# Decay attention and two MLPs on one core: masks by scans, fewer filling products in the chunk loop, operand splits ahead of weight groups

## The chip, the cores and the metric

The kernel runs on one core of one Trainium2 chip. The metric is the device time of one execution in microseconds. Engines are named as in the profile: PE is TensorE's matrix multiply and PEld its weight load, DVE is VectorE, ACT is ScalarE, POOL is GpSimd, SP is SyncE, which here issues nearly all DMAs.

## The reference

Attention with a decay per head over 2 batches, 8 heads, 768 positions and 64 channels, then two MLPs over the 1536 tokens of width 512. Everything is float32.

```python
# attention, block by block (the state runs over the blocks)
Dmask = where(i >= j, lam_h ** (i - j), 0)
out   = ((q k^T) * Dmask) v  +  (q * lam ** (i + 1)) state
state = lam ** block * state + (k * lam ** (block - 1 - i))^T v
# first MLP (d_ff 1536), then second MLP (d_ff 2048)
x = (sigmoid(x @ w_gate) * (x @ w_val)) @ w_out
x = elu(x @ w_in) @ w_out2
```

## The kernel before, in words

**Attention.** The positions are cut into six chunks of 128 (`NCH` = 6, `CH` = 128), for all heads and both batches. Two tables are made at the start, both in one SBUF tile that the trace calls `low`: `da` holds the decay mask of each head (128 x 128, eight heads, 128 x 1024 in all), and `lp` the powers of lam along the positions. Keys and values are stored with their positions reversed, so a mask is constant along anti-diagonals: entry (row r, column n) depends on r + n alone. Before the change each head's mask is read out of one row: DVE builds a row of powers for each head (`pw`, 8 partitions x 256), ACT's queue writes it to DRAM (`rows`, L296), and a DMA on SP's queue (L297) reads it back, each partition from one element further, into `da`, 512 KB.

For chunk c the pieces are: `front_mm` (L325, scores `st` for one batch, 16 matmuls), `front_post` (L331, DVE multiplies scores by `da` into `pr`), `front_pre` (ACT scales keys into `kd`, L314; POOL scales queries into `ql`, L318), `state_mm` (L338, 32 matmuls into `u`), `state_post` (DVE, `sn`), `out_mm` (L355 and, from the second chunk on, L360, into `x`, and an ACT copy `xa`). Then `build_from_psum` turns the attention output of the chunk straight into the operands of the first MLP: "11" and "22" (ACT and DVE, L171 and L172), sums (DVE, L176 and L178), and the splits of the sums into a high and a low part, "143" and "P" (ACT L181, POOL L182).

**First MLP.** Each 512 x 512 product of weights and tokens is done in blocks by seven products (M1 to M7, a Strassen scheme). One product here is a call of `step`: six matmuls of 256 columns at L209 into one of three PSUM banks A, B, C, and an eviction. A bank is taken again by the next pair as soon as its last eviction is done. A pair G (gate) or V (value) is the seven products M2, M5, M1, M4, M3, M7, M6 for one set of tokens.

**Filling products.** The pairs G and V of the first weight group are done in three parts of 256 columns: part 1 is ready after chunk 1, part 2 after chunk 3, part 3 after chunk 5. Each part puts 14 products into the list `fills`. Inside the chunk loop `fill(k)` takes k products from the list, between attention's own matmuls. What is left goes out after the loop (`fill(len(fills))`, L508). Before any product is ready, in chunks 0 and 1, `warm_up` matmuls on zeros stand there.

**Order of the work.** In the attention part PE and SP run in the written order (`manual_schedule`). The other engines, and PE after the loop, are ordered by a planner that simulates the program when it is built and takes what is ready by priority; `tc.high_priority(offset=HP)` puts instructions ahead of ordinary ones. The chunk loop's own work is in such a block, and so are the first half of `build_from_psum` and the fills. The preparation of weight groups (`prep_pair`: L71 to L73 unpack, L81 to L85 sums on POOL, L91 and L92 splits) has ordinary priority, and so have the "143" and "P" splits of `build_from_psum` (L181, L182). The split weights have two buffers of each kind, so the next gate group is split only when the first gate group has been used for the last time.

**SP's queue** in written order: lam, chunk 0, the masks (L297, waits for `rows`), the first gate weights (L61), chunks 1 and 2, the first value weights, chunks 3, 4 and 5.

Of the kernel before, what the change touches and what calls it, by code (L numbers as in the profile page):

```python
# [7 lines left out]
F32 = mybir.dt.float32  # L8
# [4 lines left out]
ALU = mybir.AluOpType  # L13
PSUM = bass.MemoryType.PSUM

P = 128
B, H, S, D = 2, 8, 768, 64
NP = H // 2
CH = 128
# [3 lines left out]
NS = (256, 512)  # L23
FG = 256
TB = 256
HP = 1000
# [4 lines left out]
def tile_decay_attention_two_mlps(  # L31
# [11 lines left out]
    nc = tc.nc  # L43
# [5 lines left out]
    sig_p = ctx.enter_context(tc.tile_pool(name="sig", bufs=1))  # L49
# [113 lines left out]
    def build_from_psum(ops, s, x0, x1, xa, t0, n, sums):  # L163


        sl = slice(t0, t0 + n)
        o = ops[s]
        a, b = slice(0, 2), slice(2, 4)
        with tc.high_priority(offset=HP):
            for key, src in (("11", x0[:, a]), ("22", x1[:, b])):  # L170
                nc.scalar.copy(o[key, "h"][:, :, sl], src)  # L171
                nc.vector.tensor_tensor(out=o[key, "l"][:, :, sl], in0=src, in1=o[key, "h"][:, :, sl].bitcast(F32),  # L172
                                        op=ALU.subtract)
            for k, (i0, i1, op) in enumerate(((x1[:, b], xa[:, a], ALU.add), (x0[:, b], xa[:, a], ALU.subtract),
                                              (x1[:, a], xa[:, 4:6], ALU.subtract))):
                nc.vector.tensor_tensor(out=sums[:, k], in0=i0, in1=i1, op=op)  # L176
            t = t_p.tile([P, 512], F32, tag="xt", name="xt", bufs=3).rearrange("p (k n) -> p k n", k=KC)
            nc.vector.tensor_tensor(out=t, in0=x1, in1=xa[:, 0:KC], op=ALU.add)  # L178
        for key, src, view in (("143", sums, (slice(None),) * 3), ("P", t, (slice(None),) * 2)):
            hi_, lo_ = (o[key, q][view + (sl,)] for q in "hl")  # L180
            nc.scalar.copy(hi_, src)  # L181
            nc.gpsimd.tensor_tensor(out=lo_, in0=src, in1=hi_.bitcast(F32), op=ALU.subtract)  # L182


    t2_p, ps1_p = [], []
# [60 lines left out]
    with ExitStack() as actx:  # L246
        a2_p = actx.enter_context(tc.tile_pool(name="a2", bufs=2))
        ap_p = actx.enter_context(tc.tile_pool(name="ap", bufs=1, space=PSUM))
        dr_p = actx.enter_context(tc.tile_pool(name="dr", bufs=1, space=bass.MemoryType.DRAM))

        start = ExitStack()
        start.enter_context(tc.manual_schedule(engines={mybir.EngineType.PE, mybir.EngineType.SP}))
# [2 lines left out]
        low = acc_p.tile([P, 2, KC, NS[0]], F32, tag="acc0", name="low").rearrange("p a k n -> p (a k n)")  # L255
        nat = acc_p.tile([P, 2, KC, NS[1]], F32, tag="acc1", name="nat").rearrange(
            "p a k n -> p (a k n)").rearrange("p (z b q h e) -> p z b q h e", z=2, b=2, q=2, h=H)
        da = low[:, 0:1024].rearrange("p (q g n) -> p q g n", q=2, g=NP)
        lp = low[:, 1024:1536].rearrange("p (g n) -> p g n", g=NP)
        rev = da[:, :, :, CH - 1:CH]  # L260
        l_ch = lp[:, :, CH - 1:CH]


        lam_s = a2_p.tile([P, 1 + NP], F32, tag="lam", name="lam", bufs=1)
        nc.sync.dma_start(out=lam_s, in_=lam2)
        pw = sig_p.tile([P, 2, 2, NS[0]], F32, tag="sig0", name="pw").rearrange("p a h n -> p (a h n)")[0:H, 0:2 * CH]
        rows = dr_p.tile([H, 2 * CH], F32, name="rows")

        tin, nat_of = {}, {c: nat[:, int(c in (1, 4))] for c in (0, 1, 3, 4, 5)}

        def load(c, halves=False):
            if c == 2:
                tin[c] = xop_p.tile([P, KC, NS[1]], F32, tag="xPh1", name="tin2").rearrange(
                    "p k n -> p (k n)").rearrange("p (b q g s) -> p b q g s", b=2, q=2, g=NP)
                nat_of[c] = sig_p.tile([P, 2, 2, NS[1]], F32, tag="sig1", name="nat2").rearrange(
                    "p a h n -> p (a h n)").rearrange("p (b q h e) -> p b q h e", b=2, q=2, h=H)
            else:
                tin[c] = a2_p.tile([P, 2, 2, NP, CH], F32, tag="tin", name="tin")
            to = tin[c].rearrange("p b q g s -> p b (q g s)")
            for b in (slice(0, 1), slice(1, 2)) if halves else (slice(0, 2),):  # L280
                nc.sync.dma_start(out=to[:, b], in_=att[c, 0][:, b])
            nc.sync.dma_start(out=nat_of[c].rearrange("p b q h e -> p b (q h e)"), in_=att[c, 1])

        load(0, True)
        nc.vector.memset(pw[:, 0:CH - 1], 0.0)
        nc.vector.memset(pw[:, CH - 1:CH], 1.0)
        nc.vector.memset(pw[:, 2 * CH - 1:2 * CH], 0.0)
        nc.vector.tensor_copy(pw[:, CH:CH + 1], lam_s[0:H, 0:1])
        n = 1
        while n < CH // 2:  # L290
            nc.vector.tensor_tensor(out=pw[:, CH + n:CH + 2 * n], in0=pw[:, CH:CH + n],
                                    in1=pw[:, CH + n - 1:CH + n].to_broadcast([H, n]), op=ALU.mult)
            n *= 2
        nc.vector.tensor_tensor(out=pw[:, CH + n:CH + 2 * n - 1], in0=pw[:, CH:CH + n - 1],
                                in1=pw[:, CH + n - 1:CH + n].to_broadcast([H, n - 1]), op=ALU.mult)
        nc.scalar.dma_start(out=rows, in_=pw)  # L296
        nc.sync.dma_start(out=da.rearrange("p q g n -> p (q g) n"),  # L297
                          in_=bass.AP(tensor=rows.tensor, offset=rows.offset, ap=[[1, CH], [2 * CH, H], [1, CH]]))
        nc.vector.tensor_copy(lp[:, :, 0], lam_s[:, 1:1 + NP])
        n = 1  # L300
        while n < CH:
            nc.vector.tensor_tensor(out=lp[:, :, n:2 * n], in0=lp[:, :, 0:n],
                                    in1=lp[:, :, n - 1:n].to_broadcast([P, NP, n]), op=ALU.mult)
# [29 lines left out]
        def state_mm(c):  # L333
            u = us[c] = ap_p.tile([P, 2, NP, D], F32, tag="u", name="u", bufs=1)
            for b in range(2):
                for p in range(NP):
                    for q, r in ((0, lo), (1, hi)):
                        nc.tensor.matmul(u[r, b, p], lhsT=kds[c][:, b, 2 * p + q], rhs=nat_of[c][:, b, 1, 2 * p + q],  # L338
                                         start=True, stop=True)

        def state_post(c):
            u = us[c]
            sn = sns[c + 1] = a2_p.tile([P, 2, NP, D], F32, tag="sn", name="sn")
            if c == 0:
                nc.vector.tensor_copy(sn, u)
            else:
                for p in range(NP):
                    nc.vector.scalar_tensor_tensor(out=sn[:, :, p], in0=sns[c][:, :, p], scalar=l_ch[:, p],
                                                   in1=u[:, :, p], op0=ALU.mult, op1=ALU.add)
# [22 lines left out]
        def fill(k):  # L372
            for _ in range(k):
                if fills:
                    fills.pop(0)()
# [6 lines left out]
        def warm_up(k):  # L382
            for _ in range(k):
                nc.tensor.matmul(warm, lhsT=idle[:, :P], rhs=idle, start=True, stop=True)
# [10 lines left out]
        for c in range(NCH):  # L395
            if c == 0:
                wV = prep_pair(w_val, 0, nc.gpsimd, nc.gpsimd)
            more = c + 1 < NCH
            with tc.high_priority(offset=HP):
                if more:  # L400
                    state_mm(c)
                    state_post(c)
                    front_pre(c + 1)
                fill(2)
                for b in range(2):
                    out_mm(c, b)
                    if c <= FIRST[0]:
                        warm_up(3)
                    fill(2)
                    if more:  # L410
                        front_mm(c + 1, b)
                        front_post(c + 1, b)
                    if c <= FIRST[0]:
                        warm_up(3)
                    fill(1 + b)
                if c + 3 < NCH and c < 2:
                    load(c + 3)
                if c == 3:
                    load(c + 2)
            if c == 1:  # L420
                xops += new_xops(1)
                sig = new_sig()
                pG = Pair("G", wG, xops, sig)
                pV = Pair("V", wV, xops, sig)
            s, t0 = (0, c * CH) if c < 2 else (1, (c - 2) * CH)
            build_from_psum(xops, s, xps[c, 0], xps[c, 1], xas[c], t0, CH,
                            a2_p.tile([P, 3, 2, CH], F32, tag="sums", name="sums"))
            if c in FIRST:
                r = PARTS[FIRST.index(c)]
                fills += [lambda q=q, m=m, r=r: step(q, m, r) for q in (pG, pV) for m in ORDER]  # L430
# [78 lines left out]
    g = new_g()  # L509
# [8 lines left out]
    for i in range(1, NG1 - 1):  # L518
# [11 lines left out]
        g = new_g()  # L530
# [15 lines left out]
    g = new_g()  # L546
# [27 lines left out]
    for i in range(NG2):  # L574
# [29 lines left out]
        if last:  # L604
            a = ws_p.tile([P, 1024, 2], U32, tag="w64", name="o64").rearrange("p (t n) x -> p t (n x)", t=4).bitcast(F32)
            b = ws_p.tile([P, 1024], F32, tag="w32", name="o32").rearrange("p (t n) -> p t n", t=2)
# [57 lines left out]
```

## Time and profile before

| | |
|---|---|
| time, median of 3 runs | 634.04 us (634.03 to 635.12) |
| the profiled execution | 633.13 us, its span on the core 631.3 us |
| PE busy | 597.9 us (95%) |
| PEld, DVE, ACT, POOL busy | 504.5 us (80%), 401.8 us (64%), 291.5 us (46%), 335.2 us (53%) |
| mean granted TensorE clock | 0.98 |
| DMA moved | 52.50 MB |

A profile's row gives the start in the span and a duration in us; behind an instruction stands in brackets how long its engine was idle before it and what released it. A window's row gives for each engine the busy time and the number of instructions, then the granted clock of TensorE (1.00 is 2.4 GHz, 0.50 is 1.2 GHz), the busy share of the DMA engines and their GB/s.

### The profile page before, as it was taken

What the parts mean: (1) busy time and instruction counts of PE and PEld (TensorE: products, weight loads), DVE (VectorE), ACT (ScalarE), POOL (GpSimd) and SP (SyncE); (2) the same over time, 40 slices, a digit from 0 to 9 for tenths busy, and PEclk for the clock granted to TensorE, in tenths of its full rate; (3) what the DMA queues carried; (4) which work ended last, traced back from release to release, by engine and by line L of the source; (5) the groups of instructions that cost most, each with busy time, mean ns of one, the idle gap of its engine ahead of it and who ended that gap; (6) DMA issues with size and microseconds to landing.
All of it is one profiled execution on the core that took longest, in us unless ns stands there. A gap on an engine that the chain in (4) does not pass through costs nothing.

```text
span 631.3 us, 9209 instructions
## 1 busy us (share of the span) xinstructions
PE 597.9 (95%) x3614; PEld 504.5 (80%) x3614; DVE 401.8 (64%) x658; ACT 291.5 (46%) x544; POOL 335.2 (53%) x262
## 2 busy tenths in 40 slices
PE   6989979999999999999999699969999999999997
PEld 3668879888888888888888588758787878788886
DVE  2867554547655566556857988554766666667574
ACT  1772235655333514515315658752727281716330
POOL 0786428777755647537427996672444545330200
PEclk8899999999999999999999889989999999999999
DMA  7953202132232121221300120321111111100004
GB/s 261 425 216 134 69 1 68 68 125 75 73 128 67 61 73 67 66 68 67 133 2 1 66 67 1 133 85 50 68 66 68 67 66 67 67 1 0 1 18 183
DMA packets 9883, 52.50 MB, mean 83 GB/s; under 512 B 1128, under 2 KB 2416, under 8 KB 4080
## 3 DMA queue, kind: packets, MB, share of 16 engines
q1 hardware_dynamic: 9824, 51.91, 22.6%
q8 instruction: 28, 0.46, 0.3%
q14 instruction: 15, 0.12, 0.1%
q10 hardware_dynamic: 16, 0.01, 0.0%
HBM read 48.76 MB, written 3.15 MB: 82 GB/s over the span
## 4 chain that ended last, share of the span: by engine, by line
PE 70%; DVE 8%; ACT 2%; POOL 2%; DMA 1%; issue 1%; ACTq 0%; SPq 0%; POOLq 0%
PE xu L482 32%; PE B L209 16%; PE A L209 16%; PE C L209 6%; DMA w<-in_w_in 1%; DVE gl L454 1%; DVE sig L235 1%; DVE acc L493 1%; DVE w L73 1%; DVE x143l L145 1%; ACT w L71 1%; DVE xt L153 1%; POOL xt L153 1%; DVE xPl L145 1%; POOL l L92 0%
## 5 line engine op out<-in xcount | busy, mean ns | idle before, releaser
L493 DVE TENSOR_TENSOR acc<-xu,acc 128x512 f32<-128x512 f32 x132 | 89.9, 688 | 69.1 <-PE xu L482 68.4
L482 PE MATMUL xu<-gh,woh 128*128 128x512 f32 (+1 forms) x322 | 125.8, 394 | 5.0 <-DVE acc L493 3.7
L482 PE MATMUL xu<-gl,woh 128*128 128x512 f32 (+1 forms) x322 | 126.8, 394 | 0.0
L482 PE MATMUL xu<-gh,wol 128*128 128x512 f32 (+1 forms) x322 | 126.1, 392 | 0.0
L454 POOL TENSOR_TENSOR gl<-sig,gh 128x1024 fp32r<-128x1024 f32 (+1 forms) x38 | 80.4, 2135 | 49.1 <-ACT gh L453 49.1
L92 POOL TENSOR_TENSOR l<-t,h 128x512 fp32r<-128x512 f32 (+1 forms) x36 | 61.2, 1702 | 36.5 <-ACT h L91 34.9
L482 PEld LDWEIGHTS xu<-gh,woh 128*128 128x128 f32 x322 | 60.8, 189 | 17.6 <-DVE acc L493 4.6
L482 PEld LDWEIGHTS xu<-gh,wol 128*128 128x128 f32 x322 | 61.2, 190 | 12.6
L482 PEld LDWEIGHTS xu<-gl,woh 128*128 128x128 f32 x322 | 61.2, 190 | 11.7 <-DVE gl L454 0.7
L92 POOL TENSOR_TENSOR l<-w,h 128x256 fp32r<-128x256 f32 x36 | 27.2, 762 | 57.9 <-ACT h L91 57.9
L453 ACT CAST gh<-sig 128x512 fp32r<-128x512 f32 (+1 forms) x58 | 44.2, 781 | 22.2 <-DVE sig L230 19.2
L73 DVE SCALAR_TENSOR_TENSOR w<-w,w 128x1024 uint32<-128x1024 uint32 x34 | 53.6, 1575 | 0.3
L91 ACT CAST h<-t 128x512 fp32r<-128x512 f32 (+1 forms) x40 | 29.0, 726 | 53.2 <-POOL t L81 28.9
L218 DVE TENSOR_TENSOR wt<-B,wt 128x256 f32<-128x256 f32 (+1 forms) x44 | 22.8, 518 | 44.2 <-PE B L209 30.4
L463 POOL TENSOR_TENSOR wol<-w,woh 128x512 fp32r<-128x512 f32 x26 | 34.5, 1350 | 27.7 <-ACT woh L461 27.7
L72 DVE TENSOR_SCALAR w<-w 128x1024 uint32<-128x1024 uint32 x34 | 32.0, 940 | 23.2 <-ACT w L71 23.2
L71 ACT ACTIVATE w<-w 128x1024 f32<-128x1024 f32 x34 | 38.5, 1132 | 15.7 <-POOL l L92 6.8
L232 ACT ACTIVATE sig<-A 128x256 f32<-128x256 f32 (+1 forms) x34 | 16.0, 471 | 63.2 <-PE A L209 37.4
L209 PE MATMUL A<-x11h,h 128*128 128x256 f32 (+1 forms) x88 | 29.9, 340 | 14.5 <-DVE sig L235 9.3
L81 POOL TENSOR_TENSOR t<-w 128x512 f32<-128x512 f32 x20 | 26.1, 1307 | 32.7 <-DVE w L73 32.7
L91 ACT CAST h<-w 128x256 fp32r<-128x256 f32 x40 | 15.8, 406 | 46.9 <-PE A L209 22.0
L233 ACT ACTIVATE sig<-sig 128x256 f32<-128x256 f32 (+1 forms) x68 | 33.9, 506 | 1.3
(135 smaller groups left out, 1540.8 us busy)
## 6 DMA issues: line engine op xcount, KB each, us to landing
w<-in_w_out SPq DMA_DIRECT2D x14, 1024.0 KB, 4.8
w<-in_w_in SPq DMA_DIRECT2D x8, 1024.0 KB, 4.7
nat<-in_att SPq DMA_DIRECT2D x6, 1024.0 KB, 8.7
w<-in_w_gate SPq DMA_DIRECT2D x6, 1024.0 KB, 5.4
w<-in_w_val SPq DMA_DIRECT2D x6, 1024.0 KB, 4.8
tin<-in_att SPq DMA_DIRECT2D x5, 1024.0 KB, 9.5
out_t<-o SPq DMA_DIRECT2D x11, 256.0 KB, 2.0
tin<-in_att SPq DMA_DIRECT2D x2, 512.0 KB, 4.8
```

The lines of the kernel that those rows point to most:

```text
L71: nc.scalar.activation(w, raw[:, :, 1].bitcast(F32), AF.Prelu, scale=2.0 ** -112, alpha=2.0 ** 32)
L72: nc.vector.tensor_scalar(out=wi, in0=wi, scalar1=3, scalar2=None, op0=ALU.logical_shift_left)
L73: nc.vector.scalar_tensor_tensor(out=wi, in0=raw[:, :, 0], scalar=29, in1=wi, op0=ALU.logical_shift_right, op1=ALU.bitwise_or)
L91: nc.scalar.copy(hi, x)
L92: eng_l.tensor_tensor(out=lo, in0=x, in1=hi.bitcast(F32), op=ALU.subtract)
L209: nc.tensor.matmul(ps, lhsT=a[:, k], rhs=b_[:, k], start=first and k == 0 and j == 0, stop=k == 1 and j == 2, skip_group_check=True,)
L233: nc.scalar.add(dst, dst, -1.0)
L453: nc.scalar.copy(h, x)
L454: ((eng0 if s == 0 else eng) or eng or nc.gpsimd).tensor_tensor(out=l, in0=x, in1=h.bitcast(F32), op=ALU.subtract)
L463: (eng or nc.gpsimd).tensor_tensor(out=lo_[:, k], in0=raw[:, k], in1=hi_[:, k].bitcast(F32), op=ALU.subtract)
L482: nc.tensor.matmul(ps, lhsT=w[:, k, cs], rhs=g_cols(g, q, k, t_)[:, bs], start=k == 0 and j == 0, stop=k == 1 and j == 2)
L493: nc.vector.tensor_tensor(out=v, in0=p, in1=v, op=ALU.add)
```

## The change

Three edits. The masks `da` are computed on DVE, one `tensor_tensor_scan` per head down the columns, x[n] = lam * x[n-1] + one[n], where `one` is an anti-diagonal of ones that POOL makes with a memset and an `affine_select`; the row of powers, its trip through DRAM and the two DMAs go, and lam is given to all partitions for all heads. The "143" and "P" splits of `build_from_psum` get high priority. In the chunk loop the fills become two after the first `out_mm` and three after the second one (none there in the last chunk), instead of 2, then 2 and 1, then 2 and 2.

```diff
@@ build_from_psum
-            nc.scalar.copy(hi_, src)
-            nc.gpsimd.tensor_tensor(out=lo_, in0=src, in1=hi_.bitcast(F32), op=ALU.subtract)
+            with tc.high_priority(offset=HP):
+                nc.scalar.copy(hi_, src)
+                nc.gpsimd.tensor_tensor(out=lo_, in0=src, in1=hi_.bitcast(F32), op=ALU.subtract)
@@ attention, start
-        lam_s = a2_p.tile([P, 1 + NP], F32, tag="lam", name="lam", bufs=1)
+        lam_s = a2_p.tile([P, H + NP], F32, tag="lam", name="lam", bufs=1)
         nc.sync.dma_start(out=lam_s, in_=lam2)
-        pw = sig_p.tile([P, 2, 2, NS[0]], F32, tag="sig0", name="pw").rearrange("p a h n -> p (a h n)")[0:H, 0:2 * CH]
-        rows = dr_p.tile([H, 2 * CH], F32, name="rows")
...
         load(0, True)
-        nc.vector.memset(pw[:, 0:CH - 1], 0.0)
...
-        nc.scalar.dma_start(out=rows, in_=pw)
-        nc.sync.dma_start(out=da.rearrange("p q g n -> p (q g) n"),
-                          in_=bass.AP(tensor=rows.tensor, offset=rows.offset, ap=[[1, CH], [2 * CH, H], [1, CH]]))
-        nc.vector.tensor_copy(lp[:, :, 0], lam_s[:, 1:1 + NP])
+        one = low[:, 1536:1536 + CH]
+        nc.gpsimd.memset(one, 1.0)
+        nc.gpsimd.affine_select(out=one, in_=one, pattern=[[1, CH]], compare_op=ALU.is_equal, fill=0.0,
+                                base=1 - CH, channel_multiplier=1)
+        for h in range(H):
+            nc.vector.tensor_tensor_scan(out=da[:, h // NP, h % NP], data0=lam_s[:, h:h + 1].to_broadcast([P, CH]),
+                                         data1=one, initial=0.0, op0=ALU.mult, op1=ALU.add)
+        nc.vector.tensor_copy(lp[:, :, 0], lam_s[:, H:H + NP])
@@ chunk loop
-                fill(2)
                 for b in range(2):
                     out_mm(c, b)
                     if c <= FIRST[0]:
                         warm_up(3)
-                    fill(2)
+                    if b == 0:
+                        fill(2)
+                    elif more:
+                        fill(3)
                     if more:
                         front_mm(c + 1, b)
                         front_post(c + 1, b)
                     if c <= FIRST[0]:
                         warm_up(3)
-                    fill(1 + b)
```

## Rows read from the trace of the kernel before

**Rows 1.** The chain that ended last, its earliest piece: start, duration, what.

```profile
92.68 0.33 DVE sums L176
```

**Rows 2.** Windows by stage: PE, PEld, DVE, ACT, POOL busy, clock, DMA.

```profile
18.26:37.01 18.75, 18.75 (x249) 12.89 (x248) 15.26 (x27) 12.79 (x35) 14.04 (x11) 0.98 1.00 408
37.01:91.10 54.09, 49.35 (x617) 43.49 (x616) 33.79 (x76) 22.45 (x53) 30.70 (x26) 1.00 0.24 86
56.01:67.53 11.52, 11.52 (x159) 10.12 (x159) 6.42 (x17) 1.51 (x4) 4.99 (x4) 1.00 0.33 104
84.63:91.10 6.47, 6.47 (x83) 5.67 (x82) 2.94 (x8) 0.86 (x2) 0.00 (x0) 1.00 0.01 3
91.10:93.75 2.65, 0.10 (x2) 0.03 (x1) 1.69 (x4) 1.35 (x3) 0.00 (x0) 1.00 0.00 0
93.75:98.00 4.25, 3.91 (x20) 3.62 (x21) 0.42 (x1) 2.46 (x6) 4.05 (x3) 0.60 0.00 0
98.00:106.00 8.00, 8.00 (x69) 8.00 (x68) 3.53 (x6) 5.49 (x14) 5.75 (x6) 1.00 0.01 3
```

**Rows 3.** Waits of PE, 36 to 110 us: total, times, longest.

```profile
PE A L209 <- DVE xt L178: 2.6, 1, 2.6
PE C L209 <- POOL x143l L182: 2.4, 1, 2.4
PE A L209 <- ACT sig L228: 2.3, 2, 1.5
```

**Rows 4.** Timeline of POOL in chunk 2.

```profile
40.10 1.43 POOL L92 TENSOR_TENSOR l<-w,h 128x256 fp32r<-128x256 f32 x2
...
42.70 1.81 POOL L182 TENSOR_TENSOR x143l<-sums,x143h 128x768 fp32r<-128x768 f32 x1
```

**Rows 5.** Timeline of all engines, first 20 us.

```profile
2.38 0.14 DVE L288 COPY pw<-lam 8x1 f32<-8x1 f32 x1 [1.10 <-DMA lam<-in_lam]
...
3.73 0.29 DVE L302 TENSOR_TENSOR low<-low 128x128 f32<-128x128 f32 x1
...
4.07 0.41 DVE L302 TENSOR_TENSOR low<-low 128x256 f32<-128x256 f32 x1
...
6.45 1.16 PE L325 MATMUL st<-tin 64*128 64x128 f32 x16
...
7.55 1.25 PE L384 MATMUL warm<-idle 128*128 128x512 bf16 x5
8.85 0.38 SPq L297 DMA_DIRECT2D low<-rows  x1
...
12.64 1.28 ACT L314 ACT_TABLE_LOAD   x1 [12.64 <-DMA low<-rows]
12.66 1.29 DVE L331 TENSOR_TENSOR pr<-st,low 128x512 f32<-128x512 f32 x2 [8.18 <-DMA low<-rows]
...
13.93 2.45 ACT L314 ACTIVATE kd<-nat,low 128x128 f32<-128x128 f32 x8
...
18.26 1.50 PE L338 MATMUL u<-nat,kd 128*64 128x64 f32 x32
```

**Rows 6.** Windows of the start, columns as in group 2.

```profile
2.00:8.00 6.00, 6.00 (x32) 2.66 (x31) 2.11 (x16) 0.00 (x0) 0.00 (x0) 1.00 0.93 321
8.00:9.00 1.00, 0.80 (x4) 0.19 (x2) 0.00 (x0) 0.00 (x0) 0.00 (x0) 1.00 0.44 182
12.24:18.26 6.02, 4.85 (x21) 2.87 (x21) 3.37 (x6) 4.75 (x10) 0.00 (x0) 0.50 0.96 396
```

**Rows 7.** Timeline of PE: first matmul of two products in a row.

```profile
83.10 0.28 PE L209 MATMUL C<-x143h,h 128*128 128x256 f32 x1
...
83.82 0.28 PE L209 MATMUL A<-x143h,h 128*128 128x256 f32 x1
```

**Rows 8.** Timelines of ACT and PE: the second weight group.

```profile
96.19 0.62 ACT L91 CAST h<-t 128x512 fp32r<-128x512 f32 x1 [1.79 <-PE B L209]
...
109.39 0.40 PE L482 MATMUL xu<-gh,woh 128*128 128x512 f32 x1
```

More of the change, by code (lines that the diff above doesn't have):

```diff
@@ L248, in tile_decay_attention_two_mlps @@
         ap_p = actx.enter_context(tc.tile_pool(name="ap", bufs=1, space=PSUM))
-        dr_p = actx.enter_context(tc.tile_pool(name="dr", bufs=1, space=bass.MemoryType.DRAM))
         start = ExitStack()
@@ L284, in tile_decay_attention_two_mlps @@
         load(0, True)
-        nc.vector.memset(pw[:, 0:CH - 1], 0.0)
[L286 to L295, printed above, removed]
-        nc.scalar.dma_start(out=rows, in_=pw)
-        nc.sync.dma_start(out=da.rearrange("p q g n -> p (q g) n"),
-                          in_=bass.AP(tensor=rows.tensor, offset=rows.offset, ap=[[1, CH], [2 * CH, H], [1, CH]]))
-        nc.vector.tensor_copy(lp[:, :, 0], lam_s[:, 1:1 + NP])
+        one = low[:, 1536:1536 + CH]
[6 more added lines that the diff above has]
+        nc.vector.tensor_copy(lp[:, :, 0], lam_s[:, H:H + NP])
         n = 1
@@ L635 @@
                     np.concatenate([heads_n(k), heads_n(v)], axis=3)], axis=1)
-    row, by_parity = np.arange(P), lam.reshape(NP, 2).T
-    lam2 = np.concatenate([by_parity.reshape(H)[row % H][:, None], by_parity[row // 64]], axis=1)
+    by_parity = lam.reshape(NP, 2).T
+    lam2 = np.concatenate([np.broadcast_to(by_parity.reshape(H), (P, H)), np.repeat(by_parity, 64, axis=0)], axis=1)
     def columns(w):
```

## The prediction

> **What bounds the kernel now.** I read the chain of waits first. Its earliest piece is at 92.68 us [rows 1]: from there on the chain leads without a break to the end, most of it through PE, and it starts where the last chunk's attention output becomes operands (sums, then the first product of part 3). So whatever lets PE reach dense MLP work earlier shortens the whole, unless the weights of the MLP are late. Then the windows by stage [rows 2]. From 98 to 106 PE is busy for 8.00 of 8.00 us at full clock: from there on there is nothing to win. Before that are three stretches. Chunks 0 and 1 (18.26 to 37.01) are full on PE, but with warm-up matmuls. The chunks from 2 on (37.01 to 91.10, 54.09 us) have PE idle for 4.74 us. Behind the loop come 2.65 us with PE nearly empty and 4.25 us at a granted clock of 0.60. The waits of PE [rows 3] name the idle times: 2.6 for the last sum, 2.4 in one piece for "x143l" on POOL, 2.3 in two pieces for a bank whose sigmoid was late. Last the timeline of the start [rows 5]: ACT and DVE wait for the mask's DMA until 12.64 and 12.66, and the first state product starts at 18.26. A reader should see that the kernel has three separate losses ahead of 98 us, and that each edit aims at one of them.
>
> **The masks.** What goes: the row of powers, two DMAs, and SP's wait. SP issued the mask's DMA at 8.85 [rows 5] and everything queued behind it (first gate weights, chunks 1 and 2) only after that; in the 8 to 9 us window the DMA engines are 0.44 busy [rows 6]. After the change these loads are issued right behind chunk 0, and the DMA stream, which is full from 12.24 on (0.96, then 1.00 for chunks 0 and 1 [rows 6, 2]), starts some 3 us earlier with 512 KB less in it. Chunk 0's own load is not faster: 321 GB/s for 6 us and 182 for 1 us make 2.1 MB, its whole size, so the keys in natural order land near 8.5 us.
>
> What comes: eight scans over 128 x 128 on DVE behind lam, which has landed at 2.38 [rows 5]. The trace has no scan. Bounds: not under 0.14 us each, the smallest DVE row of group 5 (1.1 us for eight), and at most 0.65 each, half of the 1.29 for two 128x512 multiplications (5.2 us). I take 0.41, the 128x256 multiplication, since a scan depends on its last element and should not be as quick as the 0.29 of a 128x128 one: 3.3 us. The powers `lp` were built between 2.4 and 4.5 before too (some 1.9 us of DVE). All together the masks are there at 2.4 + 3.3 + 1.9 = 7.6 us, by the bounds at 5.4 to 9.5. POOL's memset and `affine_select` start at once on an idle engine; even if both took as long as the 1.81 us of a 128x768 subtraction [rows 4] they would end near 4, which delays the scans by under 2 us and stays under the landing of the keys.
>
> [...]
>
> Now the path. ACT has the keys at 8.5, a table load of 1.28 and eight scalings of 2.45 [rows 5]: 12.2. PE's side: scores (0,0) exist at 7.6 [rows 5], mask product 1.29 from 7.6 or 9.5, scores 1.16, five warm-ups 1.25: 11.3 to 13.2. So `state_mm(0)` starts near 12.3 instead of 18.26. Before, PE also ran at 1.2 GHz (clock 0.50) from 12.24 to 18.26 [rows 6], behind a gap in which it waited for the mask; in the new order that gap is a tenth of it, and I expect 2.4 GHz throughout. Gain 6.0 (bounds 4.8 to 7). Chunks 0 and 1 are PE's own 18.75 us [rows 2], but the unpacking of the first gate weights, part of DVE's 3.37 us ahead of 18.26 [rows 6], falls into them; with all of it DVE would have 18.6 of 18.75. I deduct 0.5. **Start: -5.5 us.**
>
> **Five fills instead of nine.** One product is 83.82 - 83.10 = 0.72 us of PE [rows 7]. In the loop of before 28 are done (chunk 2: nine, 3: five, 4: nine, 5: five), after it 14. In the new order it is 5, 5, 5, 2 = 17, and 25 behind. A chunk with five products is in the trace: chunk 3, 11.52 us with PE busy throughout [rows 2]. So chunks 2, 3 and 4 take 34.6. In chunk 4 the order becomes M7, M6 of one pair and M2 of the next with nothing between; M2 needs bank A, and 2.3 us in two such waits, 0.8 and 1.5 [rows 3], price it: I add 1.0, nearer the shorter, since here an eviction has one product to hide behind. Chunk 5 is 6.47 [rows 2] less one product, 5.75. Sum 41.3 against 54.09: **loop -12.8 us.** DVE (6.42 of 11.52), ACT and POOL fit into such a chunk.
>
> Behind the loop: before, 2.65 us empty, and in the next 4.25 us 20 matmuls of 0.12, which at full clock are 2.4, so 1.85 lost. Both go, since eleven products of part 2 (7.9 us) now cover the last sums and splits. Instead 11 x 0.72 = 7.9 more work, and 1.0 for one more handover of banks (same rows as above). **Tail: +7.9 - 2.65 - 1.85 + 1.0 = +4.4 us.**
>
> **Operand splits first.** POOL ran three weight splits from 40.10 on and "x143l" only at 42.70 [rows 4], and PE stood 2.4 for it [rows 3]. With the change it goes ahead of them, and M1, its first reader, comes later in the chunk as well. This wait is inside the loop's 12.8 already. What is late instead is the first value group's split, by 3.1 us (1.81 and a little less for "P"); its first reader now stands in chunk 3, not at the end of chunk 2, so that costs nothing. Without the new fill order it could cost up to those 3 us.
>
> **What stays.** The planner lays the MLP out anew with each edit. The next weight group hangs on the last gate product of part 3: its split begins at 96.19 and the first output product runs at 109.39 [rows 8], 13.2 us later, filled by 12 remaining products and the next gate pair. The distance from that gate product to the end of the fills is unchanged, so this chain moves along.
>
> **The sum:** -5.5 - 12.8 + 4.4 = -13.9 us. On the profiled execution that is 633.13 - 13.9 = 619.2; the median of the runs is 0.9 above it, so 634.04 - 13.9, about **620 us**.
>
> **Rivals.**
> *Chunks do not shrink (0.15).* In chunk 2 ACT and POOL carry weight preparation besides. If only that chunk stays at 19 us (37.01 to the next state product at 56.01 [rows 2]), 7.5 us of the gain go: 627.6. For it: POOL's queue was the one PE waited for. Against it: five-product chunk 3 had no wait. [...]
> *The mask's transfer was covered (0.08).* If the loads of chunks 1 and 2 set the pace of the start, the 5.5 are lost: 625.6. For it: DMA is full through chunks 0 and 1. Against: PE had no wait there.
> *Slower (0.08).* 25 products now run behind the loop through one set of banks, with no attention between to cover evictions. If each waits as at a late sigmoid, PE loses per product; from 13.9 / 25 = 0.56 us each on it decides, and at 0.8, the shorter of the two waits in group 3, it costs 20 in place of the 1.0 counted above: 639. Against: 98 to 106 had the same products with no idle time.
> *The MLP takes nothing over (0.05).* If the second weight group, not PE, sets the pace, the start of the MLP is early and PE waits there: 634, no change.
> *More (0.05).* The clock and the waits fall out better, 612 to 615.
> My forecast, 616 to 624, gets 0.59. The range 615 to 629 takes in the first two rivals. A measurement of this kernel can tell about 0.2% (1.3 us) from no change: faster 0.87, same 0.05, slower 0.08.
>
> **What would show it.** Right: `state_mm(0)` near 12.3, clock 1.00 from there on, no L296 or L297; state products of chunks 2, 3, 4 some 11.5 us apart; PE without a gap behind the last `out_mm`; the first output product near 95. Wrong: a scan over 0.65 us, PE waits for `pr`, `ql` or a bank within a chunk of 13 us or more, PE gaps among the 25 products, or a later stage that loses what the first 100 us gained.

## The result

The changed kernel takes 627.14 us (median of four runs) against 634.47 for the kernel before beside it: ratio 0.9885, interval 0.9855 to 0.9915. It is 7.3 us faster; 13.9 were forecast, and 627 lies inside the range, near the edge where the rivals stand. One of the four, the one that was profiled, ran with a mean granted clock of 0.557, low in every slice of its span, and took 973.38 us, the others 625.62 to 628.01, so the rows below come from a second profile of the same kernel (run `whole_again`): 626.48 us, span 624.8, clock 0.989, against 631.3 before. The six runs of `whole_again` have a median of 625.95, 8.3 us under before.

### The profile page after: what moved, and what is told of

It reads as the page before. It is cut to its first block, busy times and chain, and to the rows that moved or that the text cites. A ratio compares the mean times of both kernels' runs of the same rounds, so it can differ in the third digit from the quotient of the medians.

```text
span 971.7 us, 9205 instructions
## 1 busy us (share of the span) xinstructions
PE 958.9 (99%) x3614; PEld 652.1 (67%) x3614; DVE 392.9 (40%) x655; ACT 298.6 (31%) x544; POOL 321.5 (33%) x264
## 4 chain that ended last, share of the span: by engine, by line
PE 98%; DVE 1%; issue 0%; ACT 0%
PE xu L474 40%; PE B L210 21%; PE A L210 21%; PE C L210 7%; PE st L316 2%; PE warm L375 2%; PE x L346 2%; PE x L351 2%; PE u L329 1%; DVE sig L236 0%; DVE w L73 0%; DVE acc L485 0%; DVE gl L446 0%; DVE sums L176 0%; DVE xt L178 0%
## 5 line engine op out<-in xcount | busy, mean ns | idle before, releaser
L474 PE MATMUL xu<-gh,wol 128*128 128x512 f32 (+1 forms) x322 | 184.7, 574 | 0.0
L474 PE MATMUL xu<-gl,woh 128*128 128x512 f32 (+1 forms) x322 | 184.6, 573 | 0.0
L474 PE MATMUL xu<-gh,woh 128*128 128x512 f32 (+1 forms) x322 | 183.2, 574 | 0.0
L474 PEld LDWEIGHTS xu<-gl,woh 128*128 128x128 f32 x322 | 73.5, 228 | 45.1 <-issue 26.7
L474 PEld LDWEIGHTS xu<-gh,wol 128*128 128x128 f32 x322 | 70.4, 219 | 48.9 <-issue 24.1
L474 PEld LDWEIGHTS xu<-gh,woh 128*128 128x128 f32 x322 | 71.7, 223 | 44.7 <-issue 26.9
L92 POOL TENSOR_TENSOR l<-t,h 128x512 fp32r<-128x512 f32 (+1 forms) x36 | 59.8, 1661 | 115.1 <-ACT h L91 109.3
L92 POOL TENSOR_TENSOR l<-w,h 128x256 fp32r<-128x256 f32 x36 | 26.3, 733 | 163.3 <-ACT h L91 154.6
L227 DVE TENSOR_TENSOR A<-A,wt 128x256 f32<-128x256 f32 (+1 forms) x44 | 23.3, 529 | 62.1 <-PE A L210 62.1
L210 PE MATMUL A<-x11h,h 128*128 128x256 f32 (+1 forms) x88 | 39.4, 448 | 8.3 <-DVE sig L236 7.3
L73 DVE SCALAR_TENSOR_TENSOR w<-w,w 128x1024 uint32<-128x1024 uint32 x34 | 44.3, 1302 | 0.2
L217 ACT COPY wt<-A 128x256 f32<-128x256 f32 (+1 forms) x44 | 19.8, 451 | 73.9 <-PE A L210 73.9
L71 ACT ACTIVATE w<-w 128x1024 f32<-128x1024 f32 x34 | 38.3, 1127 | 6.9 <-POOL l L92 4.6
```

Of the source, the lines that this page charges most:

```text
L71: nc.scalar.activation(w, raw[:, :, 1].bitcast(F32), AF.Prelu, scale=2.0 ** -112, alpha=2.0 ** 32)
L73: nc.vector.scalar_tensor_tensor(out=wi, in0=raw[:, :, 0], scalar=29, in1=wi, op0=ALU.logical_shift_right, op1=ALU.bitwise_or)
L92: eng_l.tensor_tensor(out=lo, in0=x, in1=hi.bitcast(F32), op=ALU.subtract)
L210: nc.tensor.matmul(ps, lhsT=a[:, k], rhs=b_[:, k], start=first and k == 0 and j == 0, stop=k == 1 and j == 2, skip_group_check=True,)
L227: nc.vector.tensor_tensor(out=ps, in0=ps, in1=pair.wt[r], op=ALU.add)
L474: nc.tensor.matmul(ps, lhsT=w[:, k, cs], rhs=g_cols(g, q, k, t_)[:, bs], start=k == 0 and j == 0, stop=k == 1 and j == 2)
```

## The profile after

The page's head and its busy line for PE:

```profile
span 624.8 us, 9200 instructions
...
PE 592.8 (95%) x3609; PEld 501.9 (80%) x3614; DVE 403.9 (65%) x655; ACT 292.7 (47%) x544; POOL 335.8 (54%) x264
```

PE does the same matmuls (this trace records 3609 of the 3614) and is busy for 5.1 us less; the span is 6.5 us shorter. The start, from the timeline of PE (against [rows 5]):

```profile
11.51 2.79 PE L329 MATMUL u<-nat,kd 128*64 128x64 f32 x31 [0.35 <-ACT kd L305]
...
14.09 0.28 PE L346 MATMUL x<-pr,nat 128*64 128x128 f32 x1
...
21.70 2.67 PE L316 MATMUL st<-tin 64*128 64x128 f32 x16 [2.09 <-DVE pr L322]
...
25.69 1.15 PE L329 MATMUL u<-nat,kd 128*64 128x64 f32 x32
...
35.91 1.15 PE L329 MATMUL u<-nat,kd 128*64 128x64 f32 x32
```

and from those of DVE, POOL, ACT and SP:

```profile
2.67 2.63 DVE L288 TENSOR_TENSOR_SCAN low<-lam,low 128x128 f32<-128x128 f32 x8 [1.48 <-DMA lam<-in_lam]
...
5.41 1.85 DVE L293 TENSOR_TENSOR low<-low 128x4 f32<-128x4 f32 x7
...
14.62 0.69 DVE L72 TENSOR_SCALAR w<-w 128x1024 uint32<-128x1024 uint32 x1 [3.53 <-ACT w L71]
15.35 2.18 DVE L73 SCALAR_TENSOR_TENSOR w<-w,w 128x1024 uint32<-128x1024 uint32 x1
...
18.72 2.33 DVE L92 TENSOR_TENSOR l<-w,h 128x256 fp32r<-128x256 f32 x2
20.97 1.27 DVE L322 TENSOR_TENSOR pr<-st,low 128x512 f32<-128x512 f32 x2
```

```profile
14.81 3.86 POOL L309 TENSOR_TENSOR ql<-tin,low 128x512 f32<-128x512 f32 x2 [13.44 <-DMA tin<-in_att]
```

```profile
9.76 1.28 ACT L305 ACT_TABLE_LOAD   x1 [9.76 <-DMA nat<-in_att]
11.06 2.45 ACT L305 ACTIVATE kd<-nat,low 128x128 f32<-128x128 f32 x8
13.42 1.18 ACT L71 ACTIVATE w<-w 128x1024 f32<-128x1024 f32 x1
```

```profile
2.64 0.55 SPq L61 DMA_DIRECT2D w<-in_w_gate  x1
```

Of the kernel before, three rows that [rows 5] does not have (ACT, PE, PE):

```profile
16.28 1.12 ACT L71 ACTIVATE w<-w 128x1024 f32<-128x1024 f32 x1
...
19.60 1.04 PE L355 MATMUL x<-pr,nat 128*64 128x128 f32 x16
...
26.79 1.15 PE L338 MATMUL u<-nat,kd 128*64 128x64 f32 x32
```

The masks are ready at 7.3, the keys land at 9.7, and the state products trickle behind `kd` from 11.51 to 14.2; chunk 0's first output product is at 14.09, 5.5 us ahead of before's 19.60. But chunk 1's state product, which came 8.5 us after chunk 0's before (26.79 against 18.26), now comes at 25.69: 1.1 ahead. In between PE waits 2.09 us for a mask product at 20.97. DVE had 5.2 us of unpacking and splitting the first gate weights in its queue ahead of it.

The windows by stage of `whole_again` (columns as in [rows 2]):

```profile
22.20:25.60 3.40, 2.97 (x16) 2.06 (x17) 2.27 (x7) 0.83 (x1) 0.11 (x1) 0.50 1.02 424
...
35.91:47.08 11.17, 11.17 (x159) 9.97 (x158) 7.60 (x12) 10.58 (x26) 11.17 (x11) 1.00 0.31 122
47.08:59.99 12.91, 11.72 (x161) 10.27 (x159) 12.24 (x25) 5.25 (x11) 10.85 (x11) 1.00 0.67 244
59.99:73.25 13.26, 11.41 (x160) 10.02 (x158) 8.04 (x20) 3.23 (x7) 7.76 (x6) 1.00 0.01 2
```

```profile
78.20:98.00 19.80, 19.53 (x167) 18.92 (x164) 9.63 (x21) 11.21 (x26) 10.20 (x8) 1.00 0.01 2
```

Behind the wait the clock is at 0.50 for 3.4 us. The chunks with five products take 11.17 and 12.91, then 13.26 up to chunk 5's first output product. In chunk 3 DVE is busy for 12.24 of 12.91. Behind the loop PE is busy for 19.53 of 19.80, where it stood 2.65 and then ran at 0.60 [rows 2]. The waits of PE from 35 to 110 us, which answer to [rows 3], then the longest of them in the timeline, the first product of the value pair in chunk 4:

```profile
PE A L210 <- DVE sig L231: 2.1, 2, 1.8
PE st L316 <- DVE pr L322: 1.1, 1, 1.1
```

```profile
71.25 0.39 PE L210 MATMUL A<-x11h,h 128*128 128x256 f32 x1 [1.84 <-DVE sig L231]
...
100.87 0.40 PE L474 MATMUL xu<-gh,woh 128*128 128x512 f32 x1
```

The first output product is at 100.87 instead of 109.39 [rows 8]: 8.5 us won up to there, 6.5 at the end. So something behind it gives back. "x143l" goes at 39.82 on POOL and PE no longer waits for it.

To split this by stage, the same share of PE's work is looked up in each trace: each attention or MLP matmul is worth its median distance to the next one in the kernel before (567.2 us in all). "Lost" is the start time of the matmul at which so much work is done, less that work; work 20 is in chunk 2, 120 well behind the loop.

```
work done (us)         10     20     45     50    120    end
before              17.43  20.21  25.03  25.01  31.74  64.13
whole_again         16.33  19.23  20.24  22.49  24.09  57.55
masks_only          14.87  17.65  22.46  22.44  30.10  65.75
fills_only          17.83  20.98  20.72  22.96  24.55  57.58
nine_at_new_places  14.72  17.62  22.68  22.37  27.89  57.92
late_gate_weights   11.80  16.70  21.17  23.41  25.00  58.58
no_gate_unpack      14.12  17.02  18.17  20.40  21.99  55.35
no_priority         14.85  17.75  19.64  21.88  23.49  56.62
handover_apart      14.61  17.51  17.91  17.67  19.64  49.50
```

For the whole: start -1.0 (work 20), loop and tail -6.7 (to 120), the rest +1.1. Forecast were -5.5, -8.4 and 0. One profile of a kernel can lie 2 to 3 us from its median (`nine_at_new_places`: 626.85 against 630.04), so the verdicts below go by the ratios and the table says only where.

## The experiments

**The parts alone.** `masks_only` has the masks as in the change, and fills and priority as before; `fills_only` has only the new places and number of fills; `priority_only` only this:

```diff
-            nc.scalar.copy(hi_, src)
-            nc.gpsimd.tensor_tensor(out=lo_, in0=src, in1=hi_.bitcast(F32), op=ALU.subtract)
+            with tc.high_priority(offset=HP):
+                nc.scalar.copy(hi_, src)
+                nc.gpsimd.tensor_tensor(out=lo_, in0=src, in1=hi_.bitcast(F32), op=ALU.subtract)
```

> The whole change once more, for a profile at full clock. Theory A (the start gained about what was forecast, the loop and the tail less): the first state product near 13.6 us (keys land near 9.7, table load 1.28, scalings 2.45), chunks 2 to 4 of 12 to 13.5 us each. Theory B (attention gained all that was forecast, the MLP gives some 6 us back): the first output product of the first MLP near 95 to 96 us as forecast (109.39 before), and the distance from it to the end of the span over 527 us, against 631.3 - 109.39 = 521.9 before. Time 625 to 628 in both.

> The kernel before with the scans alone; old fills, old priorities. Forecast's term: -5.5 us (ratio 0.991). Theory A: -4 to -5. Theory B: the first state product 4 to 5 us earlier and the whole less than 3 us faster.

> The kernel before with the new fill counts alone; masks by transfer, old priorities. Forecast's terms: -12.8 + 4.4 = -8.4 us (ratio 0.987), of which up to 3 could be lost to the splits that still come late. Theory A: -2 to -4. Theory B: attention ends 8 us earlier but the time falls by 2 to 4 only.

> The kernel before with high priority on the splits of the sums alone. Forecast: the wait of 2.4 us for x143l goes, but the first value group's splits come 3 us later and are read at the end of chunk 2, so 0 to -2.4 us. Both theories expect this; it bounds what this edit adds by itself.

Measured, as ratio to before, which ran beside them (634.23): whole 0.987 [0.9848, 0.9891], masks 1.0026 [1.0008, 1.0044], fills 0.9891 [0.9869, 0.9914], priority 1.0004 [0.9988, 1.0021]. The fills are the gain (-7.5 us by the medians, -6.9 by the ratio). The masks alone make it slower by 1.7 us, and on top of the fills masks and priority bring 0.8 us by the medians, 1.3 by the ratios, with overlapping intervals. PE's timeline of `masks_only`:

```profile
11.61 2.79 PE L328 MATMUL u<-nat,kd 128*64 128x64 f32 x31 [0.67 <-ACT kd L304]
...
21.80 1.75 PE L315 MATMUL st<-tin 64*128 64x128 f32 x16 [2.09 <-DVE pr L321]
...
24.23 1.15 PE L328 MATMUL u<-nat,kd 128*64 128x64 f32 x32
```

The same wait of 2.09; this time the granted clock is 1.00 from 20 to 26 us, and chunk 1 is at 24.23, 2.6 ahead of before, as in the table at work 20. Four more traces have a wait of 2.1 here and a clock of 1.00 behind it (`nine_at_new_places`, `handover_apart`, `no_priority`, `sums_first`). So the fall of the clock behind the wait (1.5 us at work 20, `whole_again` against `no_priority`) is not in every execution, but the wait is. Some of them have a stretch of 3.4 us at 0.50 elsewhere instead (`masks_only` from 42.1, `nine_at_new_places` from 41.8, `sums_first` from 71.8), `handover_apart` and `no_priority` have none before 340 us. What is left of the start, 2.6, is lost again: 0.9 up to work 120, and in the MLP 3.3, from work 120 to the end 35.7 instead of 32.4.

**Is it the weights that are early?** `late_gate_weights` issues the loads of chunks 1 and 2 ahead of the first gate weights; `no_gate_unpack` leaves out DVE's two unpacking instructions of the first gate weights; `more_warm_up` gives PE ten warm-up matmuls instead of three ahead of the wait.

```diff
@@ late_gate_weights
+        load(1)
+        load(2)
         w64 = load_w(w_gate, 0)
-        load(1)
...
-        load(2)
@@ no_gate_unpack
+        whole = raw is None
...
-        nc.vector.tensor_scalar(out=wi, in0=wi, scalar1=3, scalar2=None, op0=ALU.logical_shift_left)
...
+        if whole:
+            nc.vector.tensor_scalar(out=wi, in0=wi, scalar1=3, scalar2=None, op0=ALU.logical_shift_left)
...
@@ more_warm_up
-                        warm_up(3)
+                        warm_up(10 if (c, b) == (0, 1) else 3)
```

> The whole change, and the first gate weights are loaded behind chunks 1 and 2 (near 23 us instead of 12), so their unpacking on DVE falls out of chunk 0. Theory W (in the whole change DVE does that unpacking and splitting in chunk 0, ahead of a mask product that PE waits for): the wait of 2.1 us for pr and the fall of the clock behind it go, chunk 2 starts at 31.5 to 32.5 instead of 35.9, and the time is 3 to 4 us under the whole change, ratio to before 0.981. Rival C (chunk 0 is held by its own DVE, ACT and POOL work, or by the loads of chunk 1, not by the weights): chunk 2 starts within 1 us of 35.9 and the time does not change; it rises if the weights come too late for the first fill.

> The whole change, and DVE's two unpacking instructions of the first gate weights are left out (so these weights are wrong; 1 of 34 groups, 2.9 us of DVE in chunk 0). Theory D (the start's gain is held by the amount of weight preparation that DVE has to do between the first chunk and the first fills; moving it only moves the loss): the wait for pr in chunk 0 falls from 2.1 to under 0.5, chunk 2 starts 2 to 3 us earlier than the 34.2 to 35.9 of the other runs, and unlike with the late gate weights the gain is still there at chunk 4; time 621 to 624. Rival S (only the place in chunk 0 matters, later chunks are bound by ACT and POOL): the gain of chunk 0 is gone again by chunk 4, time as the whole change.

> The whole change with ten warm-up products instead of three behind the second output product of chunk 0, ahead of the score product that waits for pr: the wait is filled (7 x 0.27 = 1.9 us) and nothing else changes. Theory W's second half (the 2.1 us wait lets the clock fall to 1.2 GHz, which costs more than 1 us again): the clock stays at 2.4 GHz, the score product behind it takes 1.2 instead of 2.7 us, chunk 2 starts 1.5 to 2 us earlier, the time 1 to 2 us lower. Rival: the clock's fall is hidden by work that waits anyway: no change.

Measured: late 627.31 (0.9886 [0.9869, 0.9902]), no unpacking 624.33 (0.9831 [0.9807, 0.9855]), more warm-up 625.02 (0.9854 [0.9836, 0.9871]). PE in `late_gate_weights`, then DVE:

```profile
21.16 1.15 PE L330 MATMUL u<-nat,kd 128*64 128x64 f32 x32
...
30.57 0.48 PE L317 MATMUL st<-tin 64*128 64x128 f32 x2 [0.97 <-DVE pr L323]
31.54 1.16 PE L317 MATMUL st<-tin 64*128 64x128 f32 x14 [0.48 <-DVE pr L323]
```

```profile
25.52 1.52 DVE L72 TENSOR_SCALAR w<-w 128x1024 uint32<-128x1024 uint32 x1 [2.04 <-ACT w L71]
27.07 2.18 DVE L73 SCALAR_TENSOR_TENSOR w<-w,w 128x1024 uint32<-128x1024 uint32 x1
```

Chunk 0 is without a wait, and chunk 1's state product comes at 21.16, 5.6 us ahead of before: the whole forecast, for one chunk. Then the unpacking stands in chunk 1 in the same way, and by work 20 only 3.5 are left, by 45 none of it against the whole (21.17 against 20.24; from 50.6 on the clock is at 0.50 for 3.4 us). The cost moves with the weights; the time is that of the whole kernel, not the 3 to 4 us less that were expected. Without the two unpacking instructions PE still waits 1.49, where under 0.5 was expected, and the ratio is 0.0039 under the whole's, with intervals that just overlap. Just ahead of the second half of the mask product, which starts at 20.91, DVE has a later split of the same weights (L94 is L92 of the other kernels):

```profile
19.84 1.15 DVE L94 TENSOR_TENSOR l<-t,h 128x768 fp32r<-128x768 f32 x1 [0.23 <-ACT h L93]
```

So weight preparation stands ahead of the mask product in this trace too; that it is all of the wait is not shown, since no run takes out all of it. With more warm-up PE's wait is 0.6 and the clock 1.00, but chunk 1 starts at 24.36 and `no_priority`, which has the wait of 2.1 and a clock of 1.00, starts it at 24.21; the ratio is not to be told from the whole's either. So the warm-up is not shown to bring anything.

**Number or place of the fills, and the one handover.** `nine_at_new_places` does up to nine products a chunk at the two new places (nine, five, nine and four: one less than before); `handover_apart` takes one product out of chunk 4 into chunk 5, so that M2 no longer follows straight on M7 and M6.

```diff
@@ nine_at_new_places
-                        fill(2)
+                        fill(4)
-                        fill(3)
+                        fill(5)
@@ handover_apart
-                        fill(2)
+                        fill(3 if c == 5 else 2)
-                        fill(3)
+                        fill(2 if c == 4 else 3)
```

> The whole change, but four and five products at the two new places, so nine a chunk as before. Theory N (the gain comes from the number: products left over cover the end of the loop and the clock stays up there): the loop uses up its 28 again, the gap of 2.6 us and the 1.2 GHz behind it come back, and the time is 4 to 6 us above the whole change, ratio to before 0.995 to 0.998. Rival P (the gain comes from the places, which let each eviction hide behind attention's matmuls): within 2 us of the whole change.

> The whole change with one product moved: chunk 4 takes four instead of five and chunk 5 three instead of two, so that M2 of the next pair no longer follows M7 and M6 of the last one directly. The forecast priced that handover at 1.0; the trace of the whole change shows 1.84 for it. Expected: this wait goes, the time 1 to 1.8 us lower. Rival: M2 waits for the same bank later, or the wait is hidden: no change.

Measured: nine 630.04 (0.9927 [0.9905, 0.995]), apart 620.60 (0.9774 [0.9755, 0.9794]). The waits of `nine_at_new_places`, 33 to 110 us, have the three kinds of before [rows 3] again:

```profile
PE A L210 <- ACT sig L229: 2.6, 2, 1.5
PE C L210 <- POOL x143l L183: 2.3, 2, 1.9
PE A L210 <- DVE xt L178: 1.6, 1, 1.6
```

Here "x143l" has its priority and PE stands for it all the same; it was the smaller number of products that took these waits away. The gap behind the loop is back with 1.6, but the clock is 1.00 behind it, where a low one was expected. The new places count too: up to work 120 the trace is 2.2 us ahead of `masks_only` (27.89 to 30.10) with one product less in the loop, and the number brings 3.8 more (24.09), 5.4 if one counts from work 20. In the ratios the step from `masks_only` to nine is larger, 0.0099, and by the traces the rest of it is the MLP's: from 110 us on PE waits 9.1 us for sums in `masks_only` and 2.7 here. Those of `handover_apart`, 35 to 110 us:

```profile
PE st L316 <- DVE pr L322: 0.5, 1, 0.5
PE A L210 <- DVE sig L231: 0.3, 1, 0.3
```

From work 45 to 50 it loses -0.24 where the whole loses 2.25. Most of that is the 1.84 at 71.25. (Its first output product is at 96.42, near the 95 of the forecast.) But against `whole_again` the ratio is 0.0096 lower, 5 to 6 us, more than a handover. The table says where more of it is: from 120 to the end it loses 29.9, the whole 33.5. The waits of PE from 110 us on, for before, `whole_again` and `handover_apart` in turn:

```profile
PE xu L482 <- DVE acc L493: 3.7, 3, 2.4
```

```profile
PE xu L474 <- DVE acc L485: 7.6, 3, 4.7
```

```profile
PE xu L474 <- DVE acc L485: 2.7, 3, 1.4
```

The longest of the three, DVE and PE in `whole_again`, then in `handover_apart`:

```profile
412.41 2.67 DVE L72 TENSOR_SCALAR w<-w 128x1024 uint32<-128x1024 uint32 x1 [3.27 <-ACT w L71]
...
415.60 1.21 DVE L73 SCALAR_TENSOR_TENSOR w<-w,w 128x1024 uint32<-128x1024 uint32 x1
416.73 1.28 DVE L485 TENSOR_TENSOR acc<-xu,acc 128x512 f32<-128x512 f32 x2
...
417.47 0.80 PE L474 MATMUL xu<-gh,woh 128*128 128x512 f32 x1 [4.68 <-DVE acc L485]
```

```profile
408.06 2.56 DVE L72 TENSOR_SCALAR w<-w 128x1024 uint32<-128x1024 uint32 x1
410.55 0.68 DVE L485 TENSOR_TENSOR acc<-xu,acc 128x512 f32<-128x512 f32 x1
411.15 1.21 DVE L73 SCALAR_TENSOR_TENSOR w<-w,w 128x1024 uint32<-128x1024 uint32 x1
...
411.28 0.50 PE L474 MATMUL xu<-gh,woh 128*128 128x512 f32 x1 [1.40 <-DVE acc L485]
```

Same instructions, another order: in the whole kernel the planner put the first sum behind the unpacking of a weight group, in `handover_apart` between its two halves. `fills_only` has the wait of 4.7 too, so it is not the masks that bring it. An edit of one product in chunks 4 and 5 changed an order 340 us later.

**The priority and the scans once more, and the sums.** `no_priority` is the whole without the priority block; `apart_no_scans` is `handover_apart` with before's masks; `sums_first` gives the sums of the output products priority.

```diff
-                nc.vector.tensor_tensor(out=v, in0=p, in1=v, op=ALU.add)
+                with tc.high_priority(offset=HP):
+                    nc.vector.tensor_tensor(out=v, in0=p, in1=v, op=ALU.add)
```

> Scans and new fill counts without the high priority on the splits of the sums. The forecast had the wait for x143l inside the loop's term and gave the priority nothing of its own once M1 comes later in the chunk. Expected: within 1 us of the whole change. Rival: POOL's weight splits hold x143l again and the loop loses up to 2.4 us.

> New fill counts, priority, and the one product moved from chunk 4 to chunk 5 (the version of 620.6 us), but masks by transfer as before. Theory A (the scans are worth only what chunk 0 and DVE's queue leave of them): 1 to 3 us above the version with scans, 621.5 to 623.5. By the forecast's term for the start it would be 5.5 above, 626.

> The whole change with high priority on the additions of output products in the later groups (line 485) alone, so that the planner puts them ahead of weight unpacking on DVE. Theory M (the MLP gives back 1 us against before, and 3.5 against the version with one product moved, because DVE's order near 412 us puts an unpacking of 2.7 us ahead of the additions for which PE waits 4.7): the wait falls to 1.5 or less and the time by about 3 us. Rival: the new order in the whole MLP opens waits elsewhere and the time does not fall.

Measured: 627.57 (0.9875 [0.9849, 0.9902]), 621.02 (0.9768 [0.9744, 0.9791]), 627.0 (0.9876 [0.9853, 0.9899]). The priority does nothing in the whole either. Nor do the scans in the best version: 0.9768 without, 0.9774 with. With `sums_first` the longest wait for a sum fell from 4.7 to 1.8, as expected, and the median did not fall. In its trace the MLP loses 2.0 us less than the whole's, but by work 120 it had lost 0.8 more (24.88): the clock is at 0.50 for 3.4 us from 71.8 on, behind the handover's wait of 1.84. Of the 1.2 left the medians show nothing. The one wait is understood; its length is not what the kernel gains by this way of removing it.

## Why the prediction came out as it did

**The number: partly luck.** The forecast itself, 616 to 624, missed. The range held because it reached to 629 for two rivals, and neither came as told: the loop did shrink, and PE's start did move. The fills gave nearly what was forecast, the start next to nothing in time, and the MLP gave back 1.1.

**Loop and tail: right.** Forecast -8.4; `fills_only` -7.5 by its median and -8.0 in its trace from work 20 to 120. The waits for "x143l" and the last sum are gone, and PE has no gap behind the last `out_mm`. The chunks of `whole_again` are 11.17, 12.91 and 13.26 long for a forecast of 11.52; in the last of them stands the handover's wait of 1.84, and without it 11.42 would be left. Two of the prediction's own signs of being wrong showed: a chunk of over 13 with a wait for a bank, and a later stage that loses. "DVE (6.42 of 11.52), ACT and POOL fit into such a chunk" was too tight: that row is of a chunk in which DVE unpacked no weights, while in `whole_again` L72 takes 4.92 us from 44.06 on, DVE works without a break from there to a mask product of chunk 3 at 52.08, and PE waits 1.1 for that. It is the first rival in small, a chunk later than it said. The tail's 1.85 for a low clock is a term of some executions only: in `masks_only` PE waits the same 2.6 for the last sum, and the clock is 1.00 from 88 to 98.

**The handover: mis-sized.** The term of 1.0 in chunk 4 is 1.84, the one at the end of the fills 0.27 (forecast 1.0). The first lies above both waits that priced it, 0.8 and 1.5; that one product moved between the two pairs removes it shows that it was the handover.

**Operand splits first: right at nothing.** "This wait is inside the loop's 12.8 already" holds, but the priority did not bring it: `priority_only` is 1.0004 and PE still waits 2.2 for "x143l" in its trace, `fills_only` has no such wait without the priority, and in `nine_at_new_places` the wait is back with it.

**The start: the step that failed is "I deduct 0.5".** What led up to it was right: masks ready at 7.3 for 7.6, eight scans in 2.63 us for 3.3, first state product at 11.51 for 12.3, though the last matmul of it comes at 14.14, behind keys that landed at 9.7 instead of 8.5 (the first gate weights, issued at 2.64, were in flight with them; whether that is the cause was not tested) and an ACT that stays 2.45 us busy; 5.5 us gained at the first output product. But PE moved 5.5 earlier and the first gate weights only 2.9 (L71 at 13.42 instead of 16.28, behind `kd` on ACT). DVE had room for the preparation in sum (18.6 of 18.75), not in its order: 5.2 us of it now stand between 14.62 and the mask product at 20.97 (the same four operations took 3.7 before), and PE waits. The deduction measures 2.9 in `masks_only` (5.5 less the 2.6 left at work 20) and 4.4 in the whole's trace, where the clock falls as well; "I expect 2.4 GHz throughout" was wrong there for 3.4 us at 0.50 (22.20 to 25.60). `late_gate_weights` shows that another time for the pile moves the cost and doesn't remove it. This is not the rival *the mask's transfer was covered*: PE did start earlier. Yet the removal of the transfer is worth nothing that the times show.

**What stays: wrong by 1.1.** The first output product runs at 100.87, where 95 was forecast: 8.5 us won of the 13.9. "This chain moves along" holds up to there; beyond it the whole's trace loses 1.1 us net. PE waits 3.9 more for sums (7.6 against 3.7), 4.7 in one wait, and is busy at a clock of 0.50 for 7.5 us between 340 and 430 where it was for 13.3 before, an estimated 2.9 won back (half of the difference). It is the small form of the rival *the MLP takes nothing over*, by another mechanism than the second weight group. In `masks_only` the MLP loses 3.3, which is more than the start gave. `handover_apart` has the same change with a better order and the lost handover back, and its trace gains 14.6 (13.9 by the medians): start -2.7, with the clock at 1.00 behind the wait, loop and tail -9.4, MLP -2.5. That 13.9 is also the forecast's sum is chance: by `apart_no_scans` the masks, which were to bring 5.5 of it, bring nothing.

**What stays open.** Why `apart_no_scans` is as quick as `handover_apart`, though its trace is 3.6 behind at work 20 (21.15) and its span 4.3 longer: its other runs are 618.78 to 621.35 and were not profiled. The two traces are not a fair pair: the profiled run of `apart_no_scans` is the slowest of its six (622.77), that of `handover_apart` the fastest of its four (618.46, the others 620.46 to 620.77). And whether anything besides weight preparation holds the 2.09 wait.

## What to carry to other kernels

A transfer taken out of a start moves PE only as far as the slowest side pipeline moves with it (here 5.5 us at chunk 0's first output product, 1.1 at chunk 1's state product): count, per engine and in queue order, what will stand in front of the first product that PE needs, not whether its sum fits. With a planner an early edit is a new lottery for late orders worth some us here (29.9 to 35.7 between work 120 and the end), so try neighbours of an edit and judge by repeated runs. Take fewer filling products where each one stands behind an operand that is barely ready (7.5 us in `fills_only`), and keep the last of one bank's users a product away from the next (1.84 us of wait, gone in `handover_apart`).

## What the runs showed of the hardware

A scan over 128 x 128 takes about as long as a plain operation over twice the elements, 402 ns against 426 (291 for a plain one of its own size); by line and form, first 8 us of `whole_again` (busy, then mean ns):

```profile
L288 DVE TENSOR_TENSOR_SCAN low<-lam,low 128x128 f32<-128x128 f32 x8 | 2.6, 402 | 1.5 <-DMA lam<-in_lam 1.5
...
L293 DVE TENSOR_TENSOR low<-low 128x256 f32<-128x256 f32 x1 | 0.4, 426 | 0.0
L293 DVE TENSOR_TENSOR low<-low 128x128 f32<-128x128 f32 x1 | 0.3, 291 | 0.0
```

Eight in a row overlap: they take 2.63 us, 0.33 each.

Unpacking operations on DVE are mostly longer here where POOL has begun first. In `before` the 22 L73 that begin while POOL has no operation under way take 1.21 to 1.23 us, the 12 that begin within one 1.36 to 2.81; of L72 21 take 0.68 to 0.70 and 13 take 0.69 to 2.89. L73 takes 1.21 where POOL is idle (at 411.15 in `handover_apart`) and, in `whole_again`, 2.18 at 15.35, while POOL's two `ql`, begun at 14.81, take 3.86, to 18.67; a single `ql` takes 1.28 at 47.15. L72 takes 0.69 at 14.62, where it starts 0.19 ahead of POOL, and 2.67 at 412.41, where it ends 0.56 after the first row below, of POOL in `whole_again`. The second row is the longest L72 of that trace; POOL works without a break from before it to 48.43.

```profile
409.81 4.71 POOL L446 TENSOR_TENSOR gl<-sig,gh 128x1024 fp32r<-128x1024 f32 x2
44.06 4.92 DVE L72 TENSOR_SCALAR w<-w 128x1024 uint32<-128x1024 uint32 x1 [1.06 <-ACT w L71]
```

The cause is not shown: L72 reads one tile and L73 two, and rows of both are longer. Such rows stand in the start, between chunks 2 and 3, and in the MLP.

The granted clock shows in the pace of the matmuls. In `before` those of 512 columns at L482 begin 0.427 us apart where it is 0.50 (353.90 to 355.61), 1.2 columns a ns, and 0.228 apart where it is 1.00 (419.18 to 421.69), 2.2 a ns. That is what the traces have for the 1.2 and 2.4 GHz of the texts above; they give the clock itself as a share alone.
